# Attention over a key and value cache: three more pieces of keys are turned on TensorE, with two 64-row matmuls side by side

## The chip, the cores and the metric

The kernel runs on one core of one Trainium2 chip. A core has a matmul engine (TensorE, PE in the profile), three engines for elementwise work and copies (VectorE or DVE, ScalarE or ACT, GpSimd or POOL) and sixteen DMA engines. Each engine works through its own list of instructions and waits on semaphores; in this kernel SyncE (SP) issues all transfers, in one queue. The metric is the time of one execution in microseconds of the device, the lower the better. The time of a kernel is the median of its runs. The profile is of one further execution.

## The reference

```python
B, Sq, D = 8, 112, 640
H, Sk, Dh = 32, 512, 192
q = (x @ wq).reshape(B, Sq, H, Dh).transpose(0, 2, 1, 3)
scores = einsum("bhqd,bhkd->bhqk", q, k_cache) * (Dh ** -0.5)
p = softmax(scores, axis=-1)
o = einsum("bhqk,bhkd->bhqd", p, v_cache)
out = o.transpose(0, 2, 1, 3).reshape(B, Sq, H * Dh) @ wo
```

All arrays are bf16. Eight batches of 112 queries meet 32 heads with 512 keys of 192 elements each. The keys and the values are by far the largest arrays: each head of each batch has its own.

## The kernel before

**Tiling.** The 32 heads are taken in 4 rounds of 8 (`HU`). A *piece* is one batch in one round: its keys for 8 heads, and its values. There are 32 pieces, numbered in the order of work. A *step* `n` is half a piece, 4 heads of one batch; there are 64 steps, and step `n` works on piece `n // 2`. PE's work comes in named groups:

- `X`: transposes of x, seven of 128 rows each, at the start.
- `Q g, lp, c`: five matmuls (L578) that make a part of the queries of half a round (group `g`) from `xT_sb` and the weights `wq_sb`. ACT copies the result to `qr` (L583, `evQ`); DVE shifts a part into `qh` (`qc`, L600 and L601).
- `S n`: the scores of a step, `Sm` with eight matmuls over 128 rows (L623, L625) and `St` with four pairs over 64 rows each (L636, L638), where the two matmuls of a pair use the upper and the lower half of the array at the same time. The scores lie in PSUM banks 0 to 3.
- softmax of a step, in four parts: DVE finds the largest score and copies the part from PSUM to `s_sb` (`smax`, L651), ACT takes the exponential into `p_sb` (`exp`, L656), DVE takes the reciprocal of the sum (`rc`, L668) and scales (`norm`, L660). `s_sb` has three places (`NSS`), so a `smax` waits for the `exp` three parts earlier, and the next `S` waits for `smax`.
- `PT n, j`: eight transposes of p on PE (L689), copied out by ACT (j = 0) or DVE (j = 1) at L695 (`evPT`). Five late steps have it done by DMA (`TD`).
- `PVt` and `PVm`: p times values, first for 64 of the columns in two side-by-side column tiles (L718), then for the other 128 (L729); ACT copies the result to `oT_sb` (`evPV`, L739).
- `O g, m`: the product with `wo` (L751), two parts of six matmuls; DVE adds the result up in `accT` (`oacc`, L765 and L766). At the end `O6`, `OL` and `OF` (L782, L806, L831) finish the last batches, and `out` is stored.

**Keys.** The matmuls need the keys with `Dh` on the partitions, so each piece is turned. `kt` holds four turned pieces (`KS`). Pieces 2 to 31 come by a transposing DMA from HBM straight into `kt` (`load_k`, L130). The first two (`NPL = 2`) come by a plain load (`load_kn`, L165) with the keys on the partitions, and PE turns them: `k_transposes(i, u, bank, eng)` (L549) does one head with six transposes of 128x128 (L553) into one PSUM bank, and one copy of 128x768 by ACT or DVE (`evK`, L559) brings it to `kt`. The plain loads need a place: piece 0 lies in the last of the three value buffers (`vt[:, VS - 1]`), piece 1 in the place of `wo`, which is loaded later. The value load that uses that buffer, and the first load of `wo` (`load_wo`, L185), wait for these transposes.

**Order.** The order of work on each engine is written out by hand in four lists, `ORDER_PE` (L193), `ORDER_ACT`, `ORDER_DVE` and `ORDER_SP` (L499). An engine does its list strictly in order. `ORDER_SP` is the order of issue of all transfers; an issue that must wait for a buffer holds up all that stand behind it. `fill` (L874) notes who last used a PSUM bank, so that the next group in that bank waits for the copy out of it.

In the list a key group is `("K", i, u, bank, eng)`: piece, head, bank and the engine of the copy.

Of the kernel before, what the change touches and what calls it, by code (L numbers as in the profile page):

```python
# [7 lines left out]
ACTF = mybir.ActivationFunctionType  # L8
# [44 lines left out]
def build_mha_kernel(nc, x, k_cache, v_cache, wq, wo, out):  # L53
    B, SQ, D = x.shape
    _, H, SK, DH = k_cache.shape
    assert B == 8 and H == 32 and SQ == 112 and D == 640 and SK == 512 and DH == 192
    DC = D // 128
    HU = 8
# [9 lines left out]
    NPL = 2  # L68
# [17 lines left out]
    with ExitStack() as es:  # L86
# [26 lines left out]
        kn = [vt[:, VS - 1], wo_flat[:, 0:HU * 768].rearrange("p (u c) -> p u c", u=HU)]  # L113
# [28 lines left out]
        def load_v(i):  # L142
# [6 lines left out]
            if i == VS - 1:  # L149
                deps = [("KT", 0, u) for u in range(HU)]  # L150
# [34 lines left out]
        def load_wo(r):  # L185
# [4 lines left out]
            old = [("O", 2 * r - 1, m, 1) for m in range(DC)] if r else [("KT", 1, u) for u in range(HU)]  # L190
# [16 lines left out]
            ("PVt", 3, 4), ("PVt", 4, 6), ("PVm", 3), ("PVm", 4), ("S", 7), ("PT", 5, 0, 6), ("Q", 1, 3, 1, 7),  # L207
# [4 lines left out]
            ("Q", 2, 2, 2, 4), ("PT", 9, 1, 6), ("S", 12), ("PVt", 8, 4), ("PVt", 9, 6), ("PVm", 8), ("PVm", 9),  # L212
# [803 lines left out]
```

## Time and profile before

| | |
|---|---|
| median of 3 runs | 444.06 us (443.87 to 449.29) |
| the profiled execution | 442.74 us |
| its span, first to last instruction | 441.0 us |
| granted clock of TensorE, mean | 1.000 |
| transposes of keys on PE (L553) | 96 matmuls |
| loads of keys by transposing DMA | 30 of 32 pieces |
| transferred | 121.82 MB, mean 276 GB/s |

In the rows of a profile a group of instructions is given as line, engine, operation, `out<-in` with shapes and the count; behind the bar stand the busy time in us and the mean ns of one, and behind a second bar the idle time of the engine just before them and what ended it. In the order of time a row gives start and length in us, then the same names; `x6` says that six instructions are merged in it, and a bracket gives the idle time before. In the row of a stretch the first pair is the stretch and its length, and then come the busy times (with instruction counts) of PE, PEld (weight loads), DVE, ACT and POOL, the granted clock, the share of the DMA engines and GB/s. A row of waits gives who waited for whom, the us in total, how often, and the longest.

### The profile page before, as it was taken

Reading aid. Unit: us, or ns where it says so; the run is one execution under the profiler, and the core shown is the slowest. Engines: PE = TensorE matmul, PEld = TensorE weight load, DVE = VectorE, ACT = ScalarE, POOL = GpSimd, SP = SyncE. Lnnn points to the kernel's source line nnn. Section 1 sums busy time; section 2 is a strip of 40 time slices with the busy share of each in tenths; the row PEclk is TensorE's granted clock in tenths of the full one; section 3 lists DMA queues with packets and bytes.
Section 4 is the critical chain, followed back from the end, with each engine's and each line's share of the span. In section 5 each row is a group of like instructions: output and inputs, shape, how many; then the busy total and the mean of one; then the engine's idle time right before and its main releaser. Section 6 shows DMA issues by size and latency. Waiting matters only on the chain.

```text
span 441.0 us, 12923 instructions
## 1 busy us (share of the span) xinstructions
PE 430.0 (98%) x5285; PEld 312.2 (71%) x5285; DVE 350.1 (79%) x1143; ACT 339.3 (77%) x752; POOL 0.7 (0%) x6
## 2 busy tenths in 40 slices
PE   8999998999999989999999999999999999999996
PEld 6576675776677656776767766777677666776896
DVE  2379889876878877878998778979889777899962
ACT  3599899877678757987778677898868677894784
POOL 0000000000000000000000000000000000000000
PEclk9999999999999999999999999999999999999999
DMA  8999999999999999999999999999999999999972
GB/s 274 372 360 225 205 256 340 357 240 254 353 214 235 231 334 365 309 247 333 240 354 231 254 236 331 359 363 235 240 223 373 291 236 240 373 235 225 217 211 81
DMA packets 247851, 121.82 MB, mean 276 GB/s; under 512 B 195440, under 2 KB 247792, under 8 KB 247792
## 3 DMA queue, kind: packets, MB, share of 16 engines
q1 hardware_dynamic: 247792, 120.99, 110.2%
q8 instruction: 42, 0.69, 0.6%
q14 instruction: 17, 0.14, 0.1%
HBM read 70.35 MB, written 1.15 MB: 162 GB/s over the span
## 4 chain that ended last, share of the span: by engine, by line
PE 92%; DMA 5%; DVE 1%; ACT 0%; issue 0%; SPq 0%
PE ps L578 20%; PE ps L751 19%; PE ps L729 12%; PE ps L689 10%; PE ps L636 8%; PE ps L718 7%; PE ps L623 6%; PE ps L625 6%; DMA vt<-in_v_cache_dram 4%; PE ps L553 1%; DMA vt<-in_k_cache_dram 1%; DVE s_sb L651 1%; PE ps L782 1%; PE ps L806 1%; PE ps L831 0%; PE ps L539 0%
## 5 line engine op out<-in xcount | busy, mean ns | idle before, releaser
L656 ACT ACTIVATE p_sb<-s_sb,nmx 112x512 bf16<-112x512 f32 x256 | 182.7, 716 | 38.4 <-DVE s_sb L651 27.0
L651 DVE TENSOR_SCALAR_CACHE_REDUCE s_sb<-ps 112x512 f32<-112x512 f32 x256 | 168.5, 684 | 29.8 <-PE ps L638 22.0
L578 PE MATMUL ps<-xT_sb,wq_sb 128*128 128x448 bf16 x480 | 102.2, 353 | 0.9 <-ACT oT_sb L739 0.3
L751 PE MATMUL ps<-oT_sb,wo_sb 128*128 128x448 bf16 (+1 forms) x480 | 94.7, 341 | 0.0
L660 DVE TENSOR_SCALAR p_sb<-p_sb,rinv 112x512 bf16<-112x512 bf16 x256 | 81.9, 347 | 1.7
L578 PEld LDWEIGHTS ps<-xT_sb,wq_sb 128*128 128x128 bf16 x480 | 43.2, 98 | 36.6 <-issue 1.8
L751 PEld LDWEIGHTS ps<-oT_sb,wo_sb 128*128 128x128 bf16 x480 | 44.1, 98 | 32.5 <-issue 1.1
L689 PEld LDWEIGHTS ps<-ident,p_sb 112*128 112x128 bf16 x944 | 52.8, 97 | 17.3 <-DVE p_sb L660 4.3
L689 PE MATMUL ps<-ident,p_sb 112*128 112x112 bf16 x944 | 62.8, 213 | 2.1 <-DVE p_sb L660 1.6
L695 ACT ACTIVATE pT_sb<-ps 128x896 bf16<-128x896 bf16 x59 | 53.3, 909 | 14.6 <-PE ps L689 12.6
L739 ACT ACTIVATE oT_sb<-ps 128x672 bf16<-128x672 f32 x64 | 46.1, 725 | 21.7 <-PE ps L729 21.4
L583 ACT ACTIVATE qr<-ps 128x448 bf16<-128x448 f32 x96 | 50.1, 538 | 13.7 <-PE ps L578 13.1
L729 PE MATMUL ps<-pT_sb,vt 128*128 128x112 bf16 x944 | 54.5, 213 | 0.0
L729 PEld LDWEIGHTS ps<-pT_sb,vt 128*128 128x128 bf16 x944 | 47.7, 98 | 3.7 <-issue 0.2
L656 ACT ACTIVATION_READ_ACCUMULATOR p_sb<-s_sb,nmx 112x1 f32 x256 | 49.1, 192 | 0.0
L695 DVE COPY pT_sb<-ps 128x896 bf16<-128x896 bf16 x59 | 36.4, 619 | 14.3 <-PE ps L689 12.3
L623 PE MATMUL ps<-kt,qr 128*112 128x256 bf16 x128 | 35.3, 276 | 0.1
L625 PE MATMUL ps<-kt,qr 128*112 128x256 bf16 x128 | 34.9, 273 | 0.0
L623 PE MATMUL ps<-kt,qh 128*112 128x256 bf16 x128 | 34.9, 273 | 0.0
L625 PE MATMUL ps<-kt,qh 128*112 128x256 bf16 x128 | 34.9, 272 | 0.0
L718 PE MATMUL ps<-pT_sb,vt 128*64 128x112 bf16 x944 | 31.7, 215 | 2.8 <-DMA vt<-in_v_cache_dram 2.8
L718 PEld LDWEIGHTS ps<-pT_sb,vt 128*64 128x64 bf16 x944 | 25.2, 110 | 12.5 <-issue 2.9
(60 smaller groups left out, 452.7 us busy)
## 6 DMA issues: line engine op xcount, KB each, us to landing
vt<-in_v_cache_dram SPq DMA_DIRECT2D x32, 1536.0 KB, 11.1
wo_sb<-in_wo_dram SPq DMA_DIRECT2D x4, 1920.0 KB, 13.6
wq_sb<-in_wq_dram SPq DMA_DIRECT2D x14, 480.0 KB, 9.3
vt<-in_k_cache_dram SPq DMA_DIRECT2D x2, 768.0 KB, 7.7
wo_sb<-in_k_cache_dram SPq DMA_DIRECT2D x1, 1536.0 KB, 14.2
out_dram<-xT_sb SPq DMA_DIRECT2D x8, 140.0 KB, 2.2
wq_sb<-in_wq_dram SPq DMA_DIRECT2D x1, 960.0 KB, 9.4
kt<-in_x_dram SPq DMA_DIRECT2D x2, 320.0 KB, 5.2
```

What stands on the lines that cost most here:

```text
L578: mm = e.matmul(ps[:, bank, 0:SG], wq_sb[:, dc, c0:c0 + 128], xT_sb[:, dc, bh * SG:(bh + 1) * SG], start=(dc == 0), stop=(dc == DC - 1))
L583: return e.activation(qr[:, q_slot(g, lp), c, :], ps[:, bank, 0:SG], ACTF.Copy)
L623: e.matmul(ps[0:SQ, 2 * j, hs], ev, ktb[:, :, 0, cs(i)], start=(h == 0), stop=False, skip_group_check=True)
L625: mm = e.matmul(ps[0:SQ, 2 * j + 1, hs], od, ktb[:, :, 2, cs(i)], start=(h == 0), stop=False, skip_group_check=True)
L651: return e.tensor_scalar(s_sb[:, a, :].rearrange("p (e c) -> p e c", e=2), ps[0:SQ, 2 * j:2 * j + 2, h * 256:(h + 1) * 256], -scale, None, ...
L656: return e.activation(p_sb[:, k, :], s_sb[:, a, :], ACTF.Exp, bias=nmx[:, k:k + 1], scale=-1.0, accum_out=rsum[:, k:k + 1])
L660: return e.tensor_scalar(p_sb[:, k, :], p_sb[:, k, :], rinv[:, k:k + 1], None, op0=ALU.mult)
L689: mm = e.transpose(psb[:, bank, c:c + SQ], p_sb[:, (4 * n + 2 * j + h) % 8, q * 128:(q + 1) * 128], ident[0:SQ, 0:SQ])
L695: return e.activation(dst, src, ACTF.Copy) if j == 0 else e.tensor_copy(dst, src)
L718: mm = e.matmul(ps[64 * h:64 * h + 64, b0 + j, SQ:2 * SQ], vtb[:, h0 + 2 * j + h, d0:d0 + 64], pT(j, h, q), start=(q == 0), stop=(q == 3))
L729: mm = e.matmul(ps[:, b0 + j, 2 * h * SQ:(2 * h + 1) * SQ], vtb[:, h0 + 2 * j + h, d0:d0 + 128], pT(j, h, q), start=(q == 0), stop=(q == 3))
L751: mm = e.matmul(ps[:, bank_of["O", g, m, 0], 0:nc_], wo_sb[:, k, m * 128:(m + 1) * 128], oT_sb[:, g % 2, k, 0:nc_], start=(k == 0), stop=( ...
```

## The change

`NPL` goes from 2 to 5: pieces 2, 3 and 4 come by plain loads too, and their three transposing loads go. Pieces 1 and 3 lie one after the other in the place of `wo`; pieces 2 and 4 in a free part of `accT`. So the load of piece 3 waits for the transposes of piece 1, that of piece 4 for those of piece 2, the first load of `wo` for those of pieces 1 and 3, and the first `oacc` for those of pieces 2 and 4.

A key group is now a pair of heads. For each of twelve blocks of 128x128 it issues two transposes side by side, one from partitions 0 to 63 and one from 64 to 127, each with 64 moving columns of the identity, into two neighbouring PSUM banks (`bank` and `bank + 1`). Each bank holds 768 columns and is copied out by its own copy, again of 128x768, on an engine of its own. There are 4 groups for a piece, 20 in all, with 24 matmuls and 2 copies each; of the 40 copies 20 are ACT's and 20 DVE's. The groups of piece 4 write to the place of piece 0 in `kt` and wait until it has been used.

The four lists are written anew. Up to `S(10)` stand all key groups in both lists of PE; in the new one stand, beside them, 28 `Q` groups (27 before), 16 `PT` (16), and 7 `PVt` and `PVm` (6). Ahead of the first `exp` of step 0 ACT's list has 4 copies of keys, 2 of x and 8 of queries (1, 1 and 8 before). ACT does four of the copies of x and DVE three (three and four before). SP issues x ahead of the keys, and at the end `("V", 31)` ahead of the first `OUT`.

```diff
-    NPL = 2
+    NPL = 5
...
-        kn = [vt[:, VS - 1], wo_flat[:, 0:HU * 768].rearrange("p (u c) -> p u c", u=HU)]
+        kn = [vt[:, VS - 1]]
+        for i in range(1, NPL):
+            flat = wo_flat[:, 0:HU * 768] if i % 2 else acc_flat[:, 3 * D:3 * D + HU * 768]
+            kn.append(flat.rearrange("p (u c) -> p u c", u=HU))
...
             if i == VS - 1:
-                deps = [("KT", 0, u) for u in range(HU)]
+                deps = [("KT", 0, p) for p in range(LP)]
...
-            add("SP", ("KN", i, lo, hi - lo), [], emit, f"mKN{i}_{lo}", 16)
+            old = [("KT", i - 2, p) for p in range(lo // 2, hi // 2)] if i > 2 else []
+            add("SP", ("KN", i, lo, hi - lo), old, emit, f"mKN{i}_{lo}", 16)
...
-            old = [("O", 2 * r - 1, m, 1) for m in range(DC)] if r else [("KT", 1, u) for u in range(HU)]
+            old = [("O", 2 * r - 1, m, 1) for m in range(DC)] if r else [("KT", i, p) for i in range(1, NPL, 2) for p in range(LP)]
...
         ORDER_PE = [
+            ("X", 3, 2, "DVE"), ("X", 2, 7, "DVE"), ("X", 1, 3, "ACT"), ("X", 0, 2, "DVE"), ("Q", 0, 1, 0, 5),
+            ("Q", 0, 0, 2, 4), ("Q", 0, 1, 1, 3), ("Q", 0, 1, 2, 5), ("K", 0, 1, 1, "DVE", "ACT"),
+            ("K", 0, 0, 3, "ACT", "DVE"), ("Q", 0, 0, 0, 7), ("Q", 0, 0, 1, 0), ("Q", 0, 2, 2, 6), ("Q", 0, 3, 0, 3),
+            ("K", 0, 2, 6, "ACT", "DVE"), ("S", 0), ("K", 0, 3, 5, "ACT", "DVE"), ("X", 5, 7, "ACT"),
...
+            ("Q", 1, 1, 0, 0), ("K", 1, 2, 6, "ACT", "ACT"), ("K", 2, 0, 4, "ACT", "DVE"), ("S", 2),
+            ("K", 1, 3, 4, "DVE", "DVE"), ("K", 2, 2, 6, "ACT", "DVE"), ("Q", 1, 0, 2, 0),
+            ("K", 2, 3, 4, "ACT", "DVE"), ("Q", 1, 0, 1, 1), ("K", 2, 1, 6, "ACT", "DVE"), ("PT", 0, 1, 4), ("S", 3),
...
         ORDER_SP = [
+            ("X", 1), ("X", 0), ("WQ", 0, 1, 1), ("WQ", 0, 0, 1), ("KN", 0, 0, 4), ("WQ", 0, 2, 2), ("KN", 0, 4, 4),
+            ("X", 2), ("KN", 1, 0, 8), ("KN", 2, 0, 8), ("V", 0), ("V", 1), ("KN", 3, 0, 8), ("KN", 4, 0, 8),
+            ("K", 5), ("V", 3), ("V", 2), ("WQ", 1, 3, 1), ("WQ", 1, 0, 1), ("WQ", 1, 1, 1), ("WQ", 1, 2, 1),
+            ("V", 4), ("WO", 0), ("V", 5), ("K", 6), ("K", 7), ("K", 9), ("K", 8), ("V", 6), ("V", 7), ("V", 8),
...
-        def k_transposes(i, u, bank, eng):
-            def emit(e):
-                for c in range(6):
-                    mm = e.transpose(psb[:, bank, c * 128:(c + 1) * 128], kn[i][:, u, c * 128:(c + 1) * 128], ident[:, :])
-                return mm
...
+        def k_transposes(i, p, bank, engs):
+            def emit(e):
+                for x in range(12):
+                    c, u = divmod(x, 2)
+                    ends = [e.transpose(psb[:, bank + t, x * 64:(x + 1) * 64],
+                                        kn[i][64 * t:64 * t + 64, 2 * p + u, c * 128:(c + 1) * 128],
+                                        ident[64 * t:64 * t + 64, 64 * t:64 * t + 64]) for t in range(2)]
+                return tuple(ends)
+
+            add("PE", ("KT", i, p), [kn_of[i, 2 * p], kn_of[i, 2 * p + 1]], emit, ("PE", "PE2"))
+            old = [("St", 2 * (i - KS) + 1, 3)] if i >= KS else [("XT", x) for x in range(4)] if i == KS - 1 else []
+            for t in range(2):
+                def evac(e, t=t):
+                    dst = kt[:, i % KS].rearrange("p a m (u t s) -> p (a m) u t s", t=2, s=64)[:, :, 2 * p:2 * p + 2, t, :]
+                    src = psb[:, bank + t, 0:768].rearrange("p (c u s) -> p c u s", c=6, u=2)
+                    return e.activation(dst, src, ACTF.Copy) if engs[t] == "ACT" else e.tensor_copy(dst, src)
+                add(engs[t], ("evK", i, p, t), [("KT", i, p)] + old, evac)
...
-            deps = [("O", g, m, 1)] + ([("oacc", g - 2, m)] if r else [("XT", c) for c in range(4, B * SQ // 128)])
+            deps = [("O", g, m, 1)] + ([("oacc", g - 2, m)] if r else
+                                         [("XT", c) for c in range(4, B * SQ // 128)] +
+                                         [("KT", i, p) for i in range(2, NPL, 2) for p in range(LP)])
...
+            for t in range(2):
+                fill(("KT", i, p), bank + t, ("evK", i, p, t))
```

More of the change, by code (lines that the diff above doesn't have):

```diff
@@ L277, in build_mha_kernel @@
-            ("O", 7, 1, 1, 6), ("PVt", 60, 4), ("O", 7, 0, 0, 7), ("PVm", 60), ("S", 63), ("PVt", 61, 4), ("PVm", 61),
-            ("O", 7, 0, 1, 7), ("O6", 1, 0, 1), ("PT", 62, 0, 6), ("O6", 1, 1, 1), ("PT", 62, 1, 4), ("O6", 2, 0, 0),
-            ("O6", 2, 1, 0), ("OF", 1, 7), ("O6", 0, 0, 2), ("PT", 63, 0, 3), ("PT", 63, 1, 6), ("OF", 5, 0),
-            ("O6", 0, 1, 2), ("PVt", 62, 6), ("PVt", 63, 4), ("PVm", 62), ("OF", 4, 2), ("PVm", 63), ("OL", 0, 1),
-            ("OL", 0, 0), ("OL", 1, 0), ("OL", 1, 1), ("OF", 6, 5), ("OF", 7, 1)]
@@ L499, in build_mha_kernel @@
-        ORDER_SP = [
[11 rows of a table removed]
-            ("OUT", 2), ("V", 31), ("OUT", 1), ("OUT", 5), ("OUT", 3), ("OUT", 4), ("OUT", 6), ("OUT", 7)]
[3 rows of a table added]
+            ("K", 0, 2, 6, "ACT", "DVE"), ("S", 0), ("K", 0, 3, 5, "ACT", "DVE"), ("X", 5, 7, "ACT"),
[3 rows of a table added]
+            ("K", 1, 3, 4, "DVE", "DVE"), ("K", 2, 2, 6, "ACT", "DVE"), ("Q", 1, 0, 2, 0),
[7 rows of a table added]
+            ("K", 4, 3, 4, "ACT", "DVE"), ("PVt", 3, 6), ("PVm", 3), ("S", 7), ("K", 4, 1, 6, "ACT", "DVE"),
+            ("PT", 5, 0, 5), ("PT", 6, 0), ("PT", 5, 1, 7), ("Q", 2, 0, 1, 6), ("S", 8), ("Q", 2, 0, 0, 7),
@@ new lines, in build_mha_kernel @@
+            ("PVt", 24, 4), ("PVt", 25, 6), ("PVm", 24), ("PVm", 25), ("PT", 26, 0, 0), ("Q", 4, 3, 1, 1),
[3 rows of a table added]
+            ("PVt", 28, 4), ("PVm", 28), ("PVt", 27, 0), ("PT", 29, 0, 7), ("PVm", 27), ("O", 2, 4, 0, 5),
[8 rows of a table added]
+            ("S", 38), ("PVt", 34, 4), ("PVt", 35, 6), ("PVm", 34), ("PVm", 35), ("PT", 36, 0, 0), ("PT", 36, 1, 1),
[3 rows of a table added]
+            ("PVt", 37, 5), ("PVm", 37), ("S", 41), ("PT", 39, 0, 7), ("PVt", 38, 5), ("PVm", 38), ("PT", 39, 1, 4),
+            ("S", 42), ("PVt", 39, 4), ("PVm", 39), ("Q", 6, 0, 2, 7), ("PT", 40, 0, 5), ("PT", 40, 1, 6),
@@ new lines, in build_mha_kernel @@
+            ("O", 4, 1, 0, 4), ("O", 4, 1, 1, 4), ("S", 43), ("PT", 41, 0), ("PT", 41, 1, 6), ("O", 4, 0, 0, 5),
+            ("O", 4, 0, 1, 5), ("S", 44), ("PVt", 40, 4), ("PVt", 41, 6), ("PVm", 40), ("PVm", 41), ("Q", 6, 3, 0, 0),
[9 rows of a table added]
+            ("PVt", 48, 4), ("PVt", 49, 6), ("PVm", 49), ("PVm", 48), ("Q", 7, 2, 2, 1), ("PT", 50, 0, 6),
+            ("Q", 7, 1, 1, 4), ("O", 5, 3, 0, 5), ("O", 5, 3, 1, 5), ("PT", 50, 1, 6), ("S", 53), ("Q", 7, 2, 0, 4),
+            ("PT", 51, 0, 7), ("O", 5, 0, 0, 6), ("PT", 51, 1, 0), ("Q", 7, 3, 1, 5), ("O", 5, 0, 1, 6), ("S", 54),
@@ new lines, in build_mha_kernel @@
+            ("PVt", 50, 6), ("PVt", 51, 4), ("PVm", 50), ("PVm", 51), ("PT", 52, 0, 0), ("O", 5, 2, 0, 7),
[3 rows of a table added]
+            ("PT", 55, 1, 6), ("S", 57), ("PVt", 54, 4), ("PVt", 55, 6), ("PVm", 54), ("PVm", 55), ("S", 58),
[3 rows of a table added]
+            ("O", 6, 0, 1, 5), ("S", 61), ("PVt", 59, 4), ("PVt", 58, 6), ("PVm", 58), ("PVm", 59), ("S", 62),
[5 rows of a table added]
+            ("PVt", 62, 4), ("PVm", 62), ("PVt", 63, 2), ("OF", 4, 1), ("PVm", 63), ("OF", 5, 0), ("OL", 0, 0),
+            ("OL", 1, 0), ("OL", 0, 1), ("OL", 1, 1), ("OF", 6, 3), ("OF", 7, 2)]
@@ L628, in scores @@
                 add("PE", ("Sm", n, j), [("qc", n), ("smax", n - 1, 2 * j), ("smax", n - 1, 2 * j + 1)] +
-                    ([("evK", n // 2, 4 * qd + i) for i in range(4)] if n // 2 < NPL else [("K", n // 2)]), emit)
+                    ([("evK", n // 2, 2 * qd + i, t) for i in range(2) for t in range(2)] if n // 2 < NPL else [("K", n // 2)]), emit)
             for i in range(4):
```

468 lines of the change are left out of this document (228 added, 240 removed), and 146 rows, old and new, of tables (ORDER_PE, ORDER_SP).

## The prediction, made before the changed kernel was seen

> **What bounds the kernel now.** I read the page's busy times first, then the waits of PE, then busy time by stretch, then the order of time where a stretch needed it.
>
> ```profile
> span 441.0 us, 12923 instructions
> PE 430.0 (98%) x5285; PEld 312.2 (71%) x5285; DVE 350.1 (79%) x1143; ACT 339.3 (77%) x752; POOL 0.7 (0%) x6
> DMA  8999999999999999999999999999999999999972
> ...
> PE ps L718 <- DMA vt<-in_v_cache_dram: 2.8, 2, 2.0
> ```
>
> PE is busy in 430.0 of 441.0 us, and so are the DMA engines in nearly every slice: two candidates for the bound. The row of waits decides between them: for late values PE stands still 2.8 us, in two places. So PE's own work sets the time over most of the span, and the DMA stream is only just ahead of it. The shares of DVE (79%) and ACT (77%) look harmless, but they are means over the span. By stretch (us, then PE, PEld, DVE, ACT, POOL, granted clock, DMA share, GB/s):
>
> ```profile
> 0.00:5.50 5.50, 4.02 (x18) 2.55 (x19) 0.22 (x2) 1.49 (x2) 0.71 (x6) 1.00 0.60 198
> 5.50:19.00 13.50, 13.18 (x109) 8.90 (x110) 4.26 (x11) 5.62 (x10) 0.00 (x0) 1.00 1.07 362
> 19.00:76.20 57.20, 54.38 (x655) 38.63 (x653) 50.30 (x168) 53.90 (x122) 0.00 (x0) 1.00 1.19 281
> 76.20:441.00 364.80, 358.45 (x4505) 262.15 (x4505) 295.35 (x964) 278.27 (x620) 0.00 (x0) 1.00 1.11 274
> 0.00:74.50 74.50, 69.93 (x764) 48.86 (x765) 53.12 (x175) 59.30 (x130) 0.71 (x6) 1.00 1.13 287
> ...
> 19.00 0.72 ACT L656 ACTIVATE p_sb<-s_sb,nmx 112x512 bf16<-112x512 f32 x1 [1.55 <-DVE s_sb L651]
> ...
> 74.54 0.28 PE L623 MATMUL ps<-kt,qr 128*112 128x256 bf16 x1
> ...
> 75.52 0.71 ACT L656 ACTIVATE p_sb<-s_sb,nmx 112x512 bf16<-112x512 f32 x1
> ```
>
> The first exp starts at 19.00 and the last of step 9 ends at 76.2; between them ACT is busy 53.90 of 57.2 us, so it has 3.3 us free (94% busy), where PE has 2.8. Behind 76.2 ACT is busy only 278.27 of 364.8 us, PE 358.45. So the first stage is bound by ACT as much as by PE, and the rest by PE. This matters because everything that the change adds lies ahead of S(10), which starts at 74.5.
>
> **The change part by part.** Durations are those of this execution: 442.74 us, of which the span is 441.0, so 1.74 lie around it. The runs' median is 444.06, 1.3 above it; I carry that difference over.
>
> Transfers. Pieces 2, 3 and 4 leave the transposing DMA for a plain load. One piece is 1536 KB = 1.57 MB. In a stretch of plain loads and in one of transposing ones the engines moved
>
> ```profile
> 10.00:25.00 15.00, 15.00 (x122) 9.22 (x120) 5.93 (x18) 9.69 (x22) 0.00 (x0) 1.00 1.06 372
> 30.00:65.00 35.00, 33.61 (x422) 23.88 (x421) 31.18 (x108) 32.62 (x75) 0.00 (x0) 1.00 1.26 235
> ```
>
> 372 against 235 GB/s, so 4.2 us instead of 6.7 for a piece, and 3 x 2.5 = 7.4 us less on the DMA queue. On the path of this only the 2.8 us of waits for values can come back (2.0 of them in the row below), since the rest of the stream runs beside PE. With the stream 7 us shorter and PE not faster, both waits should go: -2.8. What is late next is nothing of the DMA's: the margin grows by those 7 us and by whatever PE loses.
>
> ```profile
> 162.08 0.98 PE L718 MATMUL ps<-pT_sb,vt 128*64 128x112 bf16 x32 [2.02 <-DMA vt<-in_v_cache_dram]
> ```
>
> PE, turning keys. Now 16 heads x 6 = 96 transposes, afterwards 5 pieces x 4 pairs of heads x 12 = 240 side-by-side pairs, each turning one 128x128 block with two 64-row matmuls of 64 columns. Rows for the old way, for pairs that run side by side (in the values' product two 64-column tiles share the array), and for a change between whole-array and 64-row matmuls (in the scores):
>
> ```profile
> 24.87 0.50 PE L553 MATMUL ps<-ident,vt 128*128 128x128 bf16 x6
> ...
> 25.21 0.50 PE L553 MATMUL ps<-ident,wo_sb 128*128 128x128 bf16 x6
> ...
> 57.15 0.91 PE ps L718 x32
> 58.05 1.68 PE ps L729 x32
> ...
> 17.36 0.27 PE L623 MATMUL ps<-kt,qh 128*112 128x256 bf16 x1
> 17.47 0.27 PE L625 MATMUL ps<-kt,qr 128*112 128x256 bf16 x1
> 17.67 0.31 PE L636 MATMUL ps<-kt,qr 64*112 64x256 bf16 x1
> 17.68 0.31 PE L638 MATMUL ps<-kt,qh 64*112 64x256 bf16 x1
> ...
> 18.05 0.27 PE L638 MATMUL ps<-kt,qr 64*112 64x256 bf16 x1
> 18.25 0.23 PE L553 MATMUL ps<-ident,vt 128*128 128x128 bf16 x1
> ```
>
> Six old transposes take 25.21 - 24.87 = 0.34 us, 57 ns each: 96 x 57 = 5.5 us go. Sixteen pairs of L718 take 0.91 us, 57 ns a pair, where one whole-array matmul with the same 112 columns takes 1.68 / 32 = 52 ns: a pair costs about one matmul, so it is the moving columns that count. With 64 columns that gives 52 x 64/112 = 30 ns. No row shows 64-row loads of 128 weights at that rate; the upper bound is that a pair is as slow as an old transpose or as a pair of L718, 57 ns. I take 30, since the weight loads run beside PE in every group of the page (PEld 71% against 98%). The ends are 240 x 30 = 7.2 and 240 x 57 = 13.7 us. Going into 64-row mode costs 17.67 - 17.47 = 0.20 against 0.11 of an ordinary step, coming out the same, so 0.2 us for a run of such groups. In the new list the 20 groups form 15 runs, 7 of which stand right behind an S that leaves the array in that mode anyway: 8 x 0.2 = 1.6. Net on PE: +7.2 + 1.6 - 5.5 = +3.3, at most +9.8 us, all ahead of S(10).
>
> One rule speaks against the pairs. The trace has the two matmuls of a pair 0.01 us apart (17.67 and 17.68). The Trainium skill, page "TensorE: Matmul & The Clock Gate", section "Wait — 56ns, not 53.3ns?", has a floor of about 25 ns from the start of one matmul to that of the next however few columns it has. If that held within a pair, an estimate from this page would be 240 x 50 = 12.0 us instead of 7.2, PE would come to S(10) 4.8 us later, and with the sum below that is 449; the 0.01 us speak against it, and it is a part of rival C's chance.
>
> Copies out of PSUM. Sixteen become forty, all of the same 768 columns, 20 on each of ACT and DVE where there were 8:
>
> ```profile
> L559 ACT ACTIVATE kt<-ps 128x768 bf16<-128x768 bf16 x8 | 6.2, 833 | 4.1 <-PE ps L553 4.1
> ...
> L559 DVE COPY kt<-ps 128x768 bf16<-128x768 bf16 x8 | 4.3, 550 | 7.1 <-PE ps L553 7.1
> ...
> L546 ACT ACTIVATE xT_sb<-ps 128x640 bf16<-128x640 bf16 x3 | 2.2, 718 | 1.1 <-PE ps L539 1.1
> ```
>
> ACT: 12 x 6.2/8 = 9.3 us, and one copy of x moved over from DVE, 0.7: 10.0 us, all ahead of exp(9). Of these the new list puts three copies of keys and the one of x ahead of exp(0), 3.0 us, into a stretch where ACT was busy only 5.62 of 13.5 us: hidden. The other nine, 7.0 us, fall between exp(0) and exp(9), into a stretch with 3.3 us free. If all that idle time could be filled, S(10) moves by 3.7 us; if none, by 7.0. I take 7.0: that idle time is ACT waiting for scores which a fuller list does not make earlier. ACT's delay goes on to PE, because a score reduction needs a place in s_sb that an exp frees, and the next S needs the reduction. DVE: 12 x 4.3/8 = 6.5 us, hidden by its 6.9 us idle in that stretch and the 7 it grows by. The destination's runs shrink from 128 to 64 elements; without a row I keep 550 ns, and even ACT's 833 would add 20 x 0.28 = 5.7 us, still covered; uncovered it would be an upper end of about 6 us on the same stretch.
>
> ACT's 7.0 and PE's 3.3 are not added: the later decides. PE was busy 69.93 us up to S(10) and idle 4.57. The new list has, ahead of S(10), the same work and one more Q group, PVt and PVm: 0.95 us by the row below, half of 0.91 and half of 1.68, together 2.2. Then PE reaches S(10) at 69.93 + 3.3 + 2.2 + 4.6 = 80.0, ACT at 74.5 + 7.0 = 81.5: ACT sets it. At 57 ns a pair PE would set it, at 86.5. Those 2.2 us are work done ahead, so they come off the rest.
>
> ```profile
> 45.75 0.95 PE ps L578 x5
> ```
>
> New waits on SP's queue. The load of piece 3 goes into piece 1's place and waits for its transposes, that of piece 4 for piece 2's; behind them on SP stand K(5), V(3), V(2), and the four loads of wq. The list puts the last transposes of pieces 1 and 2 around S(2) and S(3), so near 31 to 36 us. The twelve loads ahead are 11.0 MB, 30 us at 372 GB/s, so SP stands still about when the engines have run out: 1 to 4 us lost on the queue out of the 7.4 won there. First users behind it are K(5) at S(10) and wq at a Q before S(8): over 10 us of margin, hidden. Cover gone (PE 10 us earlier), it would cost those 1 to 4.
>
> Start and end. X comes before the keys, 768 KB = 2.1 us less ahead of the first Q; but S(0) still stands behind eight Q groups and four of x, so exp(0) stays at 19: 0, at best -1. At the end V(31) goes ahead of the first outputs on SP; PE's waits have no row for it: 0. The reordered rest of the lists: 0, between -1 and +3.
>
> Sum against 442.74: +7.0 (ACT ahead of S(10)) - 2.2 (work done ahead) - 2.8 (waits for values) = +2.0, so 444.7, and with the 1.3 us to the median 446.0.
>
> **The rivals.** A, the stream was the bound: all 7.4 us come out at the end, and the new lists make the ACT stage good: 444.06 - 7.4 = 436.7. For it speaks the row of nines; against it the 2.8 us. B, the other side: the two matmuls don't run side by side but one after the other, or their weight loads don't hide. Then a block costs 2 x 57 = 114 ns, 240 x 114 = 27.4 us, +23.5 on PE, S(10) at 69.93 + 23.5 + 2.2 + 4.6 = 100.2, 18.7 later than forecast: 464.7. It decides from 36 ns a pair, where PE passes ACT, and makes over 2% (453) from about 65 ns. Against it: the L718 and L638 rows. C, half of it: 57 ns a pair, S(10) at 86.5, 5 us on top: 451. D, the transfers' waits on SP are not hidden: 4 us on top, 450. E, the change does not do what it says: plain loads gain nothing as the engines wait at the two new waits; then the 2.8 stay: 448.8.
>
> **How the numbers follow.** Forecast 0.55 (442 to 449, its own range: 3.3 less if ACT's idle time fills, 3 more for the lists), A 0.12, B 0.07, C 0.14, D 0.05, E 0.07. The range of 438 to 452 leaves out B and A, 0.19. A measurement of this kernel can tell about 2% from no change, that is 435.2 and 452.9. Faster by that: the far part of A, 0.05. Slower: B and the upper third of C, 0.12. Within: 0.83.
>
> **What would show it.** Right: the first stage, up to S(10), is longer by about 7 us with ACT at 95% or more between exp(0) and exp(9); the L553 pairs start about 30 ns apart; no wait of PE for values; the span behind S(10) is shorter by 4 to 5 us. Wrong: S(10) not later than 78 (ACT was no bound), pairs at 57 or 114 ns, waits for DMA that stay, or a span behind S(10) that changes by more than the 5 us (then the lists matter more than the change).

## The result and the profile after

The changed kernel takes 445.86 us (median of 11 runs, 445.31 to 447.44). The kernel before, run beside it on the same chip, takes 443.93 (442.17 to 449.29). The ratio is 1.0058, 95% interval 1.004 to 1.0076: no difference by the bound of 2%, and a small loss that the interval separates from none. Ratios and their intervals leave out the few runs in a slower state, over 1.5% above the fastest of the same kernel; medians and ranges are of all runs. The forecast was 446.0. The profiled execution took 446.58 us. The first lines of its page:

```profile
span 444.8 us, 13773 instructions
PE 433.1 (97%) x5669; PEld 314.8 (71%) x5669; DVE 357.4 (80%) x1154; ACT 347.2 (78%) x765; POOL 0.7 (0%) x6
...
DMA  8999999999999999999999999999999999999953
```

The span grew by 3.8 us and PE's work by 3.1. But for the last two, the digits of the DMA slices are as before: this row can't tell a stream that is just in time from one with a margin. The stretches can be told apart (columns as in the prediction's rows), the first exp now at 21.36, the last of step 9 ending at 81.92, and S(10) at 80.2:

```profile
0.00:5.50 5.50, 4.42 (x33) 3.33 (x33) 0.74 (x4) 1.49 (x2) 0.70 (x6) 1.00 0.58 167
5.50:21.36 15.86, 13.14 (x170) 7.77 (x170) 4.90 (x13) 8.41 (x14) 0.00 (x0) 1.00 1.04 364
21.36:81.92 60.56, 58.22 (x1001) 42.60 (x999) 54.99 (x176) 60.31 (x134) 0.00 (x0) 1.00 1.07 322
81.92:444.80 362.88, 357.37 (x4470) 261.05 (x4468) 296.81 (x963) 276.99 (x619) 0.00 (x0) 1.00 1.10 264
0.00:80.20 80.20, 74.05 (x1186) 52.57 (x1186) 59.06 (x186) 68.49 (x144) 0.70 (x6) 1.00 1.02 322
80.20:444.80 364.60, 359.09 (x4487) 262.19 (x4484) 298.37 (x969) 278.71 (x622) 0.00 (x0) 1.00 1.11 263
```

The loss is a sum of three parts. The first exp is 2.4 us later (19.00 to 21.36). From there to the end of exp(9) it takes 3.4 us more (57.2 to 60.56), and in this stretch ACT is busy 60.31 of 60.56 us. Behind S(10) 1.9 us come back (366.5 to 364.6). 2.4 + 3.4 - 1.9 = 3.8 (2.36, 3.36 and 1.90 before rounding).

**The start.** PE's first queries, two groups of keys, the first scores and what ACT does between them and the first exp, in order of time, from the kernel after:

```profile
8.34 1.12 PE L594 MATMUL ps<-xT_sb,wq_sb 128*128 128x448 bf16 x5 [2.35 <-DMA wq_sb<-in_wq_dram]
...
12.74 0.87 PE L565 MATMUL ps<-ident,vt 64*128 64x64 bf16 x48
...
17.94 0.32 PE L639 MATMUL ps<-kt,qr 128*112 128x256 bf16 x1
18.12 0.81 ACT L576 ACTIVATE kt<-ps 128x768 bf16<-128x768 bf16 x1
...
20.07 0.81 ACT L576 ACTIVATE kt<-ps 128x768 bf16<-128x768 bf16 x1 [1.14 <-PE ps L565]
...
20.78 0.70 ACT L557 ACTIVATE xT_sb<-ps 128x640 bf16<-128x640 bf16 x1
21.36 0.72 ACT L672 ACTIVATE p_sb<-s_sb,nmx 112x512 bf16<-112x512 f32 x1
```

and the rows of the kernel before for the first queries and S(0):

```profile
9.14 7.73 PE L578 MATMUL ps<-xT_sb,wq_sb 128*128 128x448 bf16 x40 [0.29 <-DVE xT_sb L546]
...
16.70 0.27 PE L623 MATMUL ps<-kt,qr 128*112 128x256 bf16 x1
```

The queries do begin 0.8 us earlier, but S(0) begins 1.2 us later (two groups of keys now stand among the queries, and a third ahead of S(0)), and between S(0) and the first exp lie 3.4 us instead of 2.3. ACT's list has a copy of keys whose transposes stand behind S(0) on PE, and a copy of x, ahead of exp(0): the row at 20.07 shows ACT waiting 1.14 us for PE.

**The pairs.** The row at 12.74 shows two groups of keys one behind the other, 48 matmuls or 24 pairs in 0.87 us. Without the last matmul's own 0.19 us (the mean length of one L565 matmul, in the groups further down) that is 0.68 us from the first start to the last, over 23 pairs: 30 ns a pair, the two of a pair mostly 3 to 4 ns apart in the trace.

**Behind S(10).** All of PE's waits for a named releaser there (us in total, how often, the longest):

```profile
PE ps L734 <- DMA wq_sb<-p_sb: 0.4, 1, 0.4
PE ps L767 <- DMA wo_sb<-in_wo_dram: 0.3, 1, 0.3
PE ps L734 <- ACT pT_sb L711: 0.3, 1, 0.3
PE ps L734 <- ACT xT_sb L854: 0.2, 1, 0.2
PE ps L849 <- DVE accT L833: 0.2, 1, 0.2
PE ps L639 <- DVE s_sb L667: 0.2, 1, 0.2
```

The 2.8 us for values are gone. But PE stands still 5.5 us there (364.60 - 359.09) where it was 6.4 (366.50 - 360.10): only 0.9 less. The last 64.8 us of the two spans, after and then before, show where the rest is:

```profile
380.00:444.80 64.80, 59.75 (x885) 48.51 (x882) 49.10 (x162) 43.22 (x94) 0.00 (x0) 1.00 0.89 209
```

```profile
376.20:441.00 64.80, 61.16 (x895) 49.46 (x893) 49.03 (x165) 45.92 (x101) 0.00 (x0) 1.00 0.86 220
```

PE is idle 5.1 us at the end instead of 3.6. Up to there its idle time behind S(10) fell from 2.8 to 0.5 us; the end took 1.4 us back. In both kernels 3.4 us of the idle time at the end stand behind PE's last matmul; the rise is in short stalls, of which the rows above name 1.1 us more than in the kernel before (0.4 for the transposes of p by DMA, 0.3 for wo, the rest for ACT and DVE). ACT has a wait there, at 421.6, that the kernel before does not have, for the transposes of p by DMA (from the waits of ACT after 380 us):

```profile
ACT p_sb L672 <- DMA wq_sb<-p_sb: 3.3, 1, 3.3
```

### The profile page after: what moved, and what is told of

The parts are those of the page before. It is cut to its first block, busy times and chain, and to the rows that moved or that the text cites. A ratio compares the mean times of both kernels' runs of the same rounds, so it can differ in the third digit from the quotient of the medians.

```text
span 444.8 us, 13773 instructions
## 1 busy us (share of the span) xinstructions
PE 433.1 (97%) x5669; PEld 314.8 (71%) x5669; DVE 357.4 (80%) x1154; ACT 347.2 (78%) x765; POOL 0.7 (0%) x6
## 4 chain that ended last, share of the span: by engine, by line
PE 82%; ACT 7%; DMA 6%; DVE 3%; issue 1%; SPq 0%; ACTq 0%; DVEq 0%
PE ps L767 18%; PE ps L594 17%; PE ps L745 10%; PE ps L705 10%; PE ps L652 7%; PE ps L734 6%; PE ps L639 6%; PE ps L641 5%; ACT p_sb L672 3%; DMA wo_sb<-in_wo_dram 3%; DMA wq_sb<-in_wq_dram 2%; DVE s_sb L667 2%; DMA wq_sb<-p_sb 1%; ACT qr L599 1%; ACT kt L576 1%
## 5 line engine op out<-in xcount | busy, mean ns | idle before, releaser
L652 PE MATMUL ps<-kt,qr 64*112 64x256 bf16 x128 | 34.0, 291 | 0.0
L654 PE MATMUL ps<-kt,qh 64*112 64x256 bf16 x128 | 34.0, 291 | 0.0
```

The source lines that it names most:

```text
L652: m1 = e.matmul(ps[0:SQ, 2 * j, hs], ev, ktb[0:64, :, 1, cs(i)], start=False, stop=True, skip_group_check=True)
```

## The experiments

The theory after the result: ACT sets the first stage, PE the rest, and the stream of transfers has been relieved by more than the 2.8 us of waits show. Rivals: PE's pairs or DVE's copies set the first stage; or the plain loads bring nothing. Spans and stretches are those of each run's profile, and its median is set beside that of the changed kernel, 445.86 and 446.70 in two measurements. The kernel before scatters far more than the changed one (442 to 453), so ratios to it move by half a per cent from one measurement to the next: the control shows it.

**The control: the changed kernel again.** 

> The changed kernel itself, unedited, as the base of this group of runs: 445 to 447 us, first exp at 21.4, S(10) at about 80, 364 to 366 us behind it.

Measured: 446.70 us (445.08 to 447.58), ratio 0.9996 (0.9962 to 1.0031). The first exp starts at 20.8 here, 0.6 us earlier than in the first profile, S(10) at 79.6, with 364.7 us behind it. The kernel before had a median of 447.54 there, of 32 runs from 442.81 to 453.13. The same kernel that lost 0.6% now loses nothing: a ratio near 1.005 to the kernel before isn't known better than that. The scatter of the kernel before goes with its clock: of the 26 runs in the ratio, 11 had a mean granted clock of 0.998 or more and a median of 445.0, the other 15 a lower one and 447.8. Of the changed kernel's ten runs nine had 0.998 or more, and these a median of 446.6. So where the clocks agree the changed kernel is slower here too, by some 0.3%; what lowers the other's clock was not looked into.

**Eight more copies on ACT.**

```diff
-            ("Q", 1, 1, 0, 0), ("K", 1, 2, 6, "ACT", "ACT"), ("K", 2, 0, 4, "ACT", "DVE"), ("S", 2),
+            ("Q", 1, 1, 0, 0), ("K", 1, 2, 6, "ACT", "ACT"), ("K", 2, 0, 4, "ACT", "ACT"), ("S", 2),
...
```

The same for seven other groups of pieces 2 to 4; in the lists the copies move from DVE to ACT.

> The changed kernel, with eight copies of keys (pieces 2 to 4) moved from DVE to ACT; PE, transfers and all else as they are. Theory: between the first exp and the last exp of step 9 ACT is the bound (busy 60.31 of 60.56 us), so each copy costs its whole 0.78 us there: that stretch grows by 8 x 0.78 = 6.2 us to about 66.8, S(10) starts 5 to 7 us later than the changed kernel's 80.2, and the time is 445.86 + 6 = about 452, ratio to the kernel before 1.017 to 1.02. Rival, PE and its transposes are the bound and ACT only looks full: DVE gets lighter by 4.4 us, the time changes by less than 2 us, ratio 1.002 to 1.009.

Measured: 454.04 us (452.71 to 456.55), ratio 1.017 (1.0116 to 1.0223). The stretch from exp(0) to the end of exp(9):

```profile
22.59:91.51 68.92, 60.07 (x997) 43.62 (x997) 51.99 (x168) 66.14 (x142) 0.00 (x0) 0.98 0.92 277
```

The theory held, and PE is not the bound: the stretch is 8.4 us longer than in the changed kernel, for 5.8 us more on ACT and 1.9 more on PE, while DVE has 3.0 less. PE waits 7.0 us in it for ACT's copies of keys, where it waited 1.0. The 8.4 are more than ACT's work: in this execution, the slowest of the five, the granted clock was 0.50 from 76.4 to 79.8 us, which costs up to 1.7 us and accounts for most of the rise on PE. What the rest is, under 1 us, is open.

**Old transposes in the new groups.** Same groups, banks and copies, but each head of a group turned by six whole-array transposes of 128 columns.

```diff
-                for x in range(12):
-                    c, u = divmod(x, 2)
-                    ends = [e.transpose(psb[:, bank + t, x * 64:(x + 1) * 64],
+                for t in range(2):
+                    for c in range(6):
+                        mm = e.transpose(psb[:, bank + t, c * 128:(c + 1) * 128], kn[i][:, 2 * p + t, c * 128:(c + 1) * 128],
+                                         ident[:, :])
...
```

> The changed kernel, but each group turns its two heads with twelve whole-array transposes instead of twelve side-by-side pairs; same banks, copies, loads and lists. A group then takes 12 x 57 = 0.68 us instead of 0.35, less 8 x 0.2 us for changes of mode that go: PE has 5.0 us more up to S(10). Theory, ACT bound that stage: PE is idle only about 2.3 us between the first exp and the last of step 9, and somewhat more ahead of it, so 2 to 3 of the 5 us are hidden: time 447.5 to 449, ratio 1.008 to 1.011. Rival 1, PE bound it: all 5 us show, 451, ratio 1.015 or more. Rival 2, the side-by-side pairs bring nothing (what PE saves was idle anyway): under 1 us, ratio 1.004 to 1.008.

Measured: 448.93 us (448.60 to 452.25), ratio 1.0058 (1.0029 to 1.0086), 2.2 to 3.1 above the changed kernel (and 2.9 above the next experiment, which differs from the changed kernel in the place of one load and ran on the same chip), where PE has 13.7 - 7.2 - 1.6 = 4.9 us more to do by the prediction's figures. The time is the theory's; the ratio lies in the range of the second rival, but the kernel before is the less steady measure. The stretch from exp(0) to exp(9):

```profile
22.30:85.07 62.77, 61.81 (x809) 46.90 (x806) 55.43 (x176) 61.03 (x134) 0.00 (x0) 1.00 1.00 305
```

PE now is the fuller engine, 61.81 of 62.77 us, and ACT waits. S(10) comes at 83.3 instead of 79.6 to 80.2. A part of that is a later first exp (22.3). So the side-by-side pairs are worth 2 to 3 us here: ACT's bound lies only a little above PE's.

**The first weights ahead of x.**

```diff
-            ("X", 1), ("X", 0), ("WQ", 0, 1, 1), ("WQ", 0, 0, 1), ("KN", 0, 0, 4), ("WQ", 0, 2, 2), ("KN", 0, 4, 4),
+            ("WQ", 0, 1, 1), ("X", 1), ("X", 0), ("WQ", 0, 0, 1), ("KN", 0, 0, 4), ("WQ", 0, 2, 2), ("KN", 0, 4, 4),
```

> The changed kernel, with the first piece of wq issued ahead of x instead of behind it; nothing else. In the changed kernel PE waits 2.35 us for it at 6.0 to 8.3 us, and the DMA engines moved only 141 GB/s between 4 and 5 us. Theory, this wait is a part of the late first exp (21.36 against 19.00): x and the weights are both there by about 6.5 us, the first Q group starts 1.3 to 2 us earlier, and as ACT is the bound from the first exp on, the time falls by 1 to 2 us: 444 to 445, ratio 1.001 to 1.003. Rival, the first exp is set by something else (the key copies that ACT and DVE do ahead of it, or the loads of keys): the Q group starts earlier and the time stays within 0.5 us, ratio 1.005 to 1.007.

Measured: 446.05 us (445.47 to 448.05), ratio 0.9987 (0.9956 to 1.0017). The time stays, as the rival has it, but the theory was not put to the test: the first query matmul starts at 7.96 us, against 8.34 in the changed kernel and 7.83 in the control, since PE now waits 1.3 us for x instead of for weights. S(10) comes at 79.3, within what the changed lists show elsewhere (79.2 to 80.2), and the span behind it is 366.0: PE waited there for transfers that had been just in time.

```profile
PE ps L767 <- DMA wo_sb<-in_wo_dram: 1.2, 1, 1.2
...
PE ps L734 <- DMA vt<-in_v_cache_dram: 0.8, 1, 0.8
```

**The start as before.** Keys ahead of x on SP and PE, and the key copy and the copy of x behind the first two exps on ACT.

```diff
-            ("evK", 0, 2, 0), ("evK", 0, 3, 0), ("evX", 5), ("exp", 0, 0), ("exp", 0, 1), ("evQ", 0, 2, 0),
+            ("evK", 0, 2, 0), ("exp", 0, 0), ("exp", 0, 1), ("evK", 0, 3, 0), ("evX", 5), ("evQ", 0, 2, 0),
...
-            ("X", 1), ("X", 0), ("WQ", 0, 1, 1), ("WQ", 0, 0, 1), ("KN", 0, 0, 4), ("WQ", 0, 2, 2), ("KN", 0, 4, 4),
+            ("KN", 0, 0, 4), ("X", 1), ("X", 0), ("WQ", 0, 1, 1), ("WQ", 0, 0, 1), ("WQ", 0, 2, 2), ("KN", 0, 4, 4),
```

> The changed kernel with the start as it was before: the first half of piece 0's keys is loaded first, its two groups are turned while PE would else wait for the weights, and on ACT the copy of the fourth key group and one copy of x come behind the first two exps instead of ahead of them. Theory: of the 5.7 us by which S(10) is late, 2.4 are this start; first exp at 19 to 19.5, S(10) at 77.5 to 78.5, and with ACT as full as it was the stretch from the first exp to the last of step 9 grows by at most the moved copies (1.5 us): time 1 to 2.5 us under the changed kernel, 443.5 to 445. Rival, the late first exp costs nothing since ACT only shifts its work (what is moved behind the exp comes back in the full stretch): first exp earlier, S(10) the same within 0.5 us, time as the changed kernel's.

Measured: 448.02 us (446.51 to 449.73), ratio 1.0011 (0.9983 to 1.0039); 1.3 above the control on the same chip. The stretch of this kernel, and then that of the control:

```profile
20.28:82.43 62.15, 59.38 (x1008) 43.17 (x1004) 56.03 (x179) 61.60 (x135) 0.00 (x0) 1.00 1.05 318
```

```profile
20.80:81.37 60.57, 58.23 (x1001) 42.62 (x999) 55.00 (x176) 60.36 (x134) 0.00 (x0) 1.00 1.06 323
```

The first exp is 0.5 us earlier and the stretch 1.6 longer; S(10) comes 1.1 us later. The rival came nearer: the two copies that the new list puts ahead of exp(0), 1.5 us, are no waste, for behind it they cost as much in a stretch that has no room. But the start of the kernel before did not come back with its order: S(0) began at 17.95 us, not at 16.70, and the first exp at 20.3, not at 19. So only the part of the 2.4 us that these copies make was tested.

**Four copies from ACT to DVE**, on top of that start, one of each of the groups (2,1), (3,1), (4,0) and (4,1):

```diff
-("K", 2, 1, 6, "ACT", "DVE")
+("K", 2, 1, 6, "DVE", "DVE")
...
```

> The former with four copies of keys (of pieces 2 to 4) moved from ACT to DVE. Theory: ACT has 4 x 0.78 = 3.1 us less in the full stretch, DVE 2.2 more and room for it (54.99 busy of 60.56), PE becomes the bound as it was busy 58.2 there: 1 to 2.5 us less than the former, 441.5 to 443.5, so below the kernel before or even with it. Rival, DVE is what is late (its copies stand in front of the score reductions): no gain or a loss of up to 2 us against the former.

Measured: 448.68 us (448.02 to 451.28), ratio 1.0039 (1.0009 to 1.0069).

```profile
20.96:84.25 63.29, 59.85 (x1007) 43.35 (x1004) 57.72 (x183) 59.57 (x131) 0.00 (x0) 1.00 1.03 310
```

Against the former run ACT has 2.0 us less, DVE 1.7 more, and the stretch is 1.1 longer. The rival held: in the stretch ACT waits 3.0 us for DVE, where it waited 1.6. DVE was idle 5.6 us of it, but that time could not be used for copies, which by the lists stand in front of score reductions. No split better than twenty and twenty was found.

**Two pieces, new lists.** Pieces 2 to 4 come by transposing DMA again, and their groups and copies are taken out of the lists.

```diff
-    NPL = 5
+    NPL = 2
...
-            ("X", 2), ("KN", 1, 0, 8), ("KN", 2, 0, 8), ("V", 0), ("V", 1), ("KN", 3, 0, 8), ("KN", 4, 0, 8),
+            ("X", 2), ("KN", 1, 0, 8), ("K", 2), ("V", 0), ("V", 1), ("K", 3), ("K", 4),
```

> The changed kernel's lists and side-by-side transposes, but only for pieces 0 and 1: pieces 2 to 4 come by the transposing DMA again, issued where their plain loads stood, and their 12 groups and 24 copies go. Theory: ACT has 12 copies or 9.3 us less between the first exp and the last of step 9, PE 12 x 0.45 = 5.4 us less; with the late start of exp (21.4) unchanged S(10) starts at 75 to 77 instead of 80.2, and up to 3 us of waits for values or keys come back behind it: time 442 to 445, ratio 0.996 to 1.002, so two of the changed kernel's added microseconds come from pieces 2 to 4. Rival, the new order of the lists is what costs: the time stays at 445.5 to 446.5, ratio 1.004 or more.

Measured: 452.73 us (451.44 to 453.38), ratio 1.0132 (1.0094 to 1.017). Theory and rival both missed: PE stands still for weights. The second round's, 4.8 us of the row, stand on SP behind V(2) and V(3) and landed at 69.8 us and later; the other waits in it are those of the start.

```profile
PE ps L586 <- DMA wq_sb<-in_wq_dram: 6.8, 3, 4.8
```

**Two pieces, and one load of weights ahead of V(2) and V(3).**

```diff
-("K", 5), ("V", 3), ("V", 2), ("WQ", 1, 3, 1), ("WQ", 1, 0, 1), ("WQ", 1, 1, 1), ("WQ", 1, 2, 1),
+("K", 5), ("WQ", 1, 0, 1), ("V", 2), ("V", 3), ("WQ", 1, 2, 1), ("WQ", 1, 1, 1), ("WQ", 1, 3, 1),
```

> Pieces 2 to 4 by the transposing DMA as in the run of that name, with the first of the second round's weight loads issued ahead of V(2) and V(3), so that PE does not wait for it. In the former run PE waited 4.8 us there, and its S(10) came at 85.1. Theory: that wait, a queueing of the transfers behind 3 x 2.5 us more of transposing, was the whole loss; without it the relief of ACT shows: S(10) at 78 to 80, time 1 to 3 us under the changed kernel's, 443 to 445. Rival, pieces 2 to 4 by plain load are worth more than their copies cost, because the whole stream (values too) is late: other waits for DMA take the place, time 447 or more.

Measured: 450.58 us (449.45 to 452.18), ratio 1.0091 (1.0056 to 1.0125). The rival held. S(10) comes at 76.9, 2.7 us earlier than in the control: that is the price of the twelve groups and their copies. K(5), the load right behind those of pieces 2 to 4, landed at 59.8 instead of 51.9: the plain loads of three pieces do take some 7.9 us off the stream (7.4 foreseen). And the span behind S(10) is 373.3 instead of 364.7, with this wait at S(12):

```profile
96.15 0.43 PE L620 MATMUL ps<-kt,qr 128*112 128x256 bf16 x1 [6.48 <-DMA kt<-in_k_cache_dram]
```

The keys are K(6), landed at 96.0. In the new list of SP they stand behind the weights, V(4), wo and V(5), which waits for a value buffer; in the kernel before they stand ahead of all these and landed at 67.7, needed at 85.6.

**The series in between:** five, four and three pieces, all with that load of weights ahead, run side by side. With five only those seven issues on SP change, in the way just shown; with four also:

```diff
-    NPL = 5
+    NPL = 4
...
-("KN", 3, 0, 8), ("KN", 4, 0, 8),
+("KN", 3, 0, 8), ("K", 4),
```

With three, `NPL = 3`, `("K", 3)` stands in the place of `("KN", 3, 0, 8)` too.

> The changed kernel with one move on SP, the load WQ(1,0) ahead of V(2) and V(3): the end of a series with 5, 4, 3 and 2 pieces turned on PE, all with this move (2 pieces: 450.6). The changed kernel showed no wait of PE for these loads, so both theories expect 446 to 447.5.

> Piece 4 comes by the transposing DMA again, its four key groups and eight copies are gone (5 of ACT's copies, 4.1 us, and 3 of DVE's; 2.9 us of pairs on PE); the rest of the new lists stands. Theory: relief of the stream has no threshold, each piece that stays on the plain load is worth a third of the 8.6 us behind S(10) and costs a third of the 2.7 us ahead of it: 2.0 us slower than with five pieces, 448 to 449.5, PE waiting 2 to 3 us more behind S(10). Rival: only the last part of the lag makes a stall, since values and keys wait in buffers; with a third of the lag the buffers still cover it, and the copies saved come out: 1 to 3 us faster than with five pieces, 444 to 446, span behind S(10) at 364 to 366.

> Pieces 3 and 4 come by the transposing DMA, their eight key groups and sixteen copies are gone. Theory (no threshold): two thirds of the way to the kernel with two pieces, 449 to 450, span behind S(10) at 369 to 371. Rival (threshold): at most a third of that stall, 445 to 448, S(10) 1 to 2.5 us earlier and behind it at most 368.

Measured: 446.15 us with five pieces (445.13 to 448.29, ratio 1.0035, 1.0012 to 1.0058), 445.99 with four (445.48 to 447.63, 1.0027, 1.0002 to 1.0051), 446.72 with three (444.80 to 449.82, 1.0049, 1.0025 to 1.0073); the kernel before 444.77. By the profiled spans:

| pieces turned on PE | S(10) at | behind S(10) | PE idle there | K(6) landed | S(12) wanted it at |
|---|---|---|---|---|---|
| 5 | 79.2 | 364.0 | 4.9 | 90.5 | 91.8 |
| 4 | 78.8 | 365.1 | 6.0 | 92.6 | 91.5 |
| 3 | 78.6 | 366.4 | 7.0 | 92.4 | 91.3 |
| 2 | 76.9 | 373.3 | 12.1 | 96.0 | 89.7 |

Piece 4 has four copies on each engine, not five and three as the expectation has it (ACT's instructions fall from 765 to 761). The last row is of the run above, on another chip. The rival came nearer: from five to three pieces the time hardly moves, and the stall comes in full only at two. But its gain did not come: four pieces were to be 1 to 3 us faster than five. With three pieces the same wait reads

```profile
92.54 0.29 PE L321 MATMUL ps<-kt,qr 128*112 128x256 bf16 x1 [1.22 <-DMA kt<-in_k_cache_dram]
```

For each piece from three to five 1.1 to 1.3 us come back behind S(10) and 0.2 to 0.5 are lost ahead of it; what is left by these profiles, 0.7 to 1.1 us a piece, the medians don't show. Also, with fewer pieces ACT's copies go and the stretch shrinks less than they took: with three pieces ACT is busy 54.6 of 59.1 us, where with five it was 60.4 of 60.6. So ACT is not the bound there any more; which engine is was not tried.

**Is it the place of K(6)?** Two pieces as above, K(6) ahead of V(5).

```diff
-("WO", 0), ("V", 5), ("K", 6), ("K", 7)
+("WO", 0), ("K", 6), ("V", 5), ("K", 7)
```

> The kernel with two pieces and WQ(1,0) ahead (450.6), with one move more on SP: K(6) ahead of V(5), behind which it stood and which waits for a value buffer. Theory: what the plain loads of pieces 2 to 4 bought in the new lists is the place of K(6) alone; there it landed at 96.0 and PE came to S(12) at 89.7. One transfer of values earlier (4 to 6 us) it lands at 90 to 92: PE waits 0 to 2.5 us instead of 6.5, the clock behind the wait does not fall, and the time is 444 to 447. Rival: the stream as a whole is too long for these lists, and the wait goes to K(7), V(5) or wo: span behind S(10) still 371 or more, 449 to 451.

Measured: 450.42 us (five of six runs from 449.33 to 451.83, the sixth 487.67), ratio 1.0135 (1.0073 to 1.0197). The rival held. PE's waits:

```profile
PE ps L575 <- DMA wq_sb<-in_wq_dram: 3.0, 3, 1.5
PE ps L715 <- DMA vt<-in_v_cache_dram: 2.8, 1, 2.8
PE ps L620 <- DMA kt<-in_k_cache_dram: 2.6, 1, 2.6
```

K(6) came 5 us earlier and its wait fell from 6.5 to 2.6 us, as the theory had it, but V(5) behind it landed 7 us later, PE waited for values instead, and the span behind S(10) stayed at 372.6. Three kernels with two pieces pay at three places, weights (span 449.7), K(6) (450.2) or keys and values (448.3): with these lists the stream itself is too long there, and the medians are 4 to 7 us above those with five pieces (445.86 to 446.70).

## Why the prediction was right, and where its terms were not

The time and the verdict came out; of the three terms of the sum, +7.0 - 2.2 - 2.8, only the last did, and a fourth was left at zero. That 446.0 and 445.86 lie 0.1 us apart is luck: between the two profiled executions the sum was to be +2.0 and was +3.8, and the 1.3 us by which the one before lay under its median had become 0.7 us above it after.

**"+7.0 (ACT ahead of S(10))": the engine was right, the size was not.** The prediction named both ends, 3.7 if ACT's idle time fills and 7.0 if none of it does, and took 7.0 because "that idle time is ACT waiting for scores which a fuller list does not make earlier". It filled: ACT is busy 99.6% of the stretch, which grew by 3.4 us for 6.4 more of ACT's work (53.90 to 60.31). This step failed: an ACT that runs behind no longer waits for scores, because the scores are there when it gets to them. In that stretch of the kernel before ACT waited 3.2 us for score reductions, in five places; in the changed kernel no wait of ACT is left. That ACT is the bound was right: eight more copies on it, 5.8 us, made the stretch 8.4 us longer, up to 1.7 of it by a lower clock. The Trainium skill says in "TensorEngine Tiling (Array Packing)", section "PSUM Bottleneck", that tiling speeds up TensorE and not the evacuation of PSUM, which may become the limit; the 99.6% and the longer stretch agree.

**"exp(0) stays at 19: 0, at best -1": wrong, +2.4.** The prediction counted that the copies put ahead of exp(0) fit into ACT's idle time there (8.41 us busy now, 5.62 before) and didn't follow the order: one of them waits for transposes behind S(0), and exp(0) waits behind that copy. That makes 1.1 of the 2.4 us; the other 1.2 are S(0) itself, which comes later behind the weights and the groups of keys. Moving the copies back won nothing, so their part is ACT's bill paid in advance; whether the part of S(0) can be had back is open. With the same start the first exp lay at 20.4 to 21.4 us in seven profiles (and at 22.6 and 23.4 in two whose clock was halved in the start), so the 2.4 is known to 1 us only. Both together, 2.4 + 3.4 = 5.7 by the unrounded figures, are the measured size of the term of 7.0: two errors of opposite sign, of which the sum is off by 1.3.

**"-2.8 (waits for values)": right, 2.3.** No wait for values is left, and PE's idle time between S(10) and the last 65 us fell by 2.3 us.

**"-2.2 (work done ahead)": the work went, the time did not.** PE has 39 instructions fewer behind S(10) (4526 to 4487; the prediction's Q, PVt and PVm are 5 + 16 + 16 = 37), and its busy time falls by 1.0 us, not by 2.2. And in the last 64.8 us, where PE's work fell by 1.4, its idle time rose by as much. The prediction looked at the end only for V(31) and the outputs and set it to 0; it did not ask whether the end waits for PE at all. What sets the end was not tried; ACT's 3.3 us for the transposes by DMA are one candidate, the softmax of the last steps another. So the two terms of -5.0 together gave -1.9.

**"The margin grows by those 7 us": wrong in kind.** The relief is real: take it back in these lists and 4 to 7 us are lost at each of the three places tried. But the new lists spent it. K(6) lands 1.3 to 3.1 us before S(12) with five pieces, where it had 18 in the kernel before. A stream that is just in time has a margin at each buffer, and the list on SP deals it out.

**Right in mechanism and size:** 30 ns a pair (foreseen 30, ends 30 and 57); PE was the second bound, close behind, since the old transposes cost 2 to 3 of their 4.9 us; DVE's copies at 550 ns in spite of the shorter runs (551 in the last row below), hidden as long as twenty copies are all that DVE gets; the waits of SP for pieces 3 and 4, whose loads it issued at 33.5 and 37.2 us, hidden: K(5) landed at 52.3 for S(10) at 80.2. They were hidden with less room than the prediction's "over 10 us of margin": the weights of the query group ahead of S(8) landed at 65.9 us and PE began that group at 68.0, and with two pieces it was these weights that came too late.

```profile
L565 PE MATMUL ps<-ident,vt 64*128 64x64 bf16 x96 | 1.9, 190 | 0.0
...
L576 ACT ACTIVATE kt<-ps 128x768 bf16<-128x768 bf16 x20 | 16.0, 812 | 2.5 <-PE ps L565 2.4
L576 DVE COPY kt<-ps 128x768 bf16<-128x768 bf16 x20 | 10.8, 551 | 8.6 <-PE ps L565 8.6
```

The rule on the floor of 25 ns between starts, in the Trainium skill's "TensorE: Matmul & The Clock Gate", section "Wait — 56ns, not 53.3ns?", does not hold between two halves of the array: 3 to 4 ns in most pairs, and 30 for the pair, not 50.

So of the rivals B and C fell with the 30 ns a pair, D with loads that were there in time, if by 2 us, E with the waits for values that went. A, the stream as the bound, is true of these lists with two pieces, and was not true of the kernel before.

What stays open: why the lists of the kernel before get by with two pieces (366.5 behind S(10), 74.5 ahead of it) was read from the place of K(6) and not tried, and no version was found that beats the kernel before. It has the shorter first stage, since 24 copies fewer go through ACT and DVE (2.7 us in the new lists) and its first scores come earlier, and a stream that its own order had already hidden but for 2.8 us of waits.

## What to carry to other kernels

A transfer that is made cheaper is worth no more than the waits that it causes now; here 7.4 us of stream could return 2.8, while the copies that replace it went to the engine that sets that stage. An engine's idle time in a stage that it nearly bounds should be priced at both ends, since a new order of the engine that feeds it can fill it. And work that is done ahead counts as time only if the end of the kernel waits for the engine that it was taken from.

## What the runs showed of the hardware

**The clock behind a stall.** In the kernel with two pieces and the late K(6), PE stood still from 89.7 to 96.1 us. The stall, the 5.15 us behind it and the stretch after that (the seventh value of a row is the granted clock):

```profile
89.70:96.10 6.40, 0.00 (x0) 0.00 (x0) 0.63 (x2) 1.55 (x5) 0.00 (x0) 0.75 1.19 239
96.10:101.25 5.15, 5.10 (x69) 4.37 (x69) 2.38 (x9) 0.00 (x0) 0.00 (x0) 0.65 1.21 274
101.25:112.00 10.75, 10.75 (x110) 7.45 (x107) 8.55 (x28) 9.35 (x21) 0.00 (x0) 1.00 1.23 218
```

The 0.65 is a mean: the clock was 0.50 up to 99.7 us and 1.00 behind that. Over 5.15 us it costs some 1.8 us, so a stall of 6.5 costs about 8.3 (an estimate from these rows). The waits of up to 2.8 us in the kernel with K(6) earlier left its clock at 1.00. The Trainium skill, "TensorE: Matmul & The Clock Gate", section "What's actually happening", has the clock halve after about 3.4 us of idleness and recover after about as much work; these two kernels agree. It need not be one stall: with eight more copies on ACT the clock was 0.50 from 76.4 to 79.8 us, and no stall ahead of that was longer than 1.3 us; PE was busy 1.8 of the 3.4 us before it fell.

**Where the stream starts thin.** The kernel before has keys first in the queue, the changed one x and weights. Its transfers between 4 and 5 us:

```profile
4.00:5.00 1.00, 1.00 (x15) 0.91 (x13) 0.01 (x1) 0.00 (x0) 0.00 (x0) 1.00 0.70 141
```

and of the kernel before, in that microsecond:

```profile
4.00:5.00 1.00, 1.00 (x6) 0.45 (x3) 0.00 (x0) 0.00 (x0) 0.00 (x0) 1.00 1.06 395
```

That is 141 against 395 GB/s, and the weights for the first queries came 2.35 us after PE was ready. It is not the small loads as such, and not the same each time: the control, the same kernel, moved 304 GB/s in that microsecond, with a wait of 0.8 us, and the kernel with one load of weights ahead of x, with the same small loads at the head, 392. What makes the difference is open.
